# Sliding-window attention followed by a two-matrix feed-forward layer: w_in's first columns in smaller pieces, w_out's products spread over more slots, and 512-token blocks in the middle of the loop

## The chip, the cores and the metric

The kernel runs on one core of a Trainium2 chip. A core has engines that run side by side, each with its own instruction queue: TensorE (PE in the profile; PEld is its weight load), VectorE (DVE), ScalarE (ACT), GpSimd (POOL) and SyncE (SP). They meet through semaphores. POOL, SP and ACT also issue DMA transfers. The metric is device time in microseconds (us), the median of several runs. Before the change it is 308.66 us (three runs, 308.59 to 308.95).

## What is computed

`q`, `k`, `v` have 8 batches, 8 heads, 576 positions and head size 64. The attention output, as 4608 tokens of 512 features, goes through two matrices with an activation between them.

```python
def _attn_ref(q, k, v):                       # window = 32, scale = 1 / sqrt(64)
    scores = scale * np.matmul(q, k.transpose(0, 1, 3, 2))
    mask = np.abs(pos[:, None] - pos[None, :]) <= window
    scores = np.where(mask, scores, -1000000000.0)
    attn = np.exp(scores - np.max(scores, axis=-1, keepdims=True))
    attn = attn / (np.sum(attn, axis=-1, keepdims=True) + 1e-09)
    return np.matmul(attn, v)

def _moe_ref(x, w_in, w_out):                 # w_in 512 x 2048, w_out 2048 x 512
    h = x @ w_in
    g = np.where(h >= 1, h, np.where(h <= -1, 0.0, (h + 1) ** 2 / 4))
    return g @ w_out
```

All inputs and the output are float32; the kernel computes its matmuls in bfloat16 and accumulates in float32.

## The kernel before, in words

**Tokens and slots.** The 4608 tokens are 18 blocks of 256 (`TB`), the 2048 hidden features 8 groups of 256 (`NF`). The main loop (L492) goes through 144 *slots* `a`, with block `t = a // 8` and feature group `f = a % 8`. A slot projects its block onto its 256 features: `project` (L484 to L489), eight matmuls of 256 columns into one PSUM tile `hp` (`[128, 2, 256]`, two feature halves). ACT makes `rr = relu(0.5 h + 0.5)` (L520), DVE `mx = max(h, rr)` (L527) and `gT = min(rr, 1) * mx` (L528), the activated features in bfloat16. (Seven early slots do one of the three steps on ACT.) `hp` has two buffers, `rr` and `mx` three, `gT` a tile per block from a pool of three.

**Second matrix.** `quarter(x)` (L426) does a quarter of a 128-token output tile: four matmuls over four of the 16 feature chunks, 512 columns wide. After the fourth quarter ACT copies the PSUM tile to `osb` and SP issues the store. In slot `a` from 18 on, quarter `a - 8` stands after the projection; eight slots more (144 to 151) finish. The first two blocks go through `pair` (L454), in two column halves, since w_out arrives in two halves; the last tile is split into two column halves too (L429 to L441).

**Attention.** Each batch takes five *sessions*, placed into slots by the list `sl` (L410, L411) through `at`. A session is `sums` (weighted values and row sums for a part of the rows that were scored before; L266) followed by `scores` or `scores8` of the next part (L212, L239), all in 64 x 64 matmuls. ACT takes the exponential of the scores (L236, L261), DVE applies the band mask (L202), ACT makes the reciprocal of the sums by Ln and Exp (L300, L301), and DVE multiplies it in and writes `xT` (L306, L309). That multiplication is put off by `flush` to the start of the next slot's DVE work. `xT` is a ring of four batches (2304 tokens). Within a batch the five sessions sum, in order: two head halves below column 224, two from there to column 480, and the tail (480 to 575).

**Order.** The order on every engine is that of the program (`manual_schedule`); semaphores are put in for data and buffers. Around slot `a`: `flush`, the projection, ACT and DVE on it, the session if there is one (`run(a)`), the quarter. So PE's stream is projection, session, products, and ACT's is `rr`, exp, Ln, Exp, a copy if a tile ended, next `rr`.

**Loads.** Everything from HBM but the first `q` is loaded by POOL, with the cast to bfloat16 in the transfer, in the order of L122 to L158: first k, v of batch 0, w_in's columns 0 to 511 as two transfers (one for each half of the partitions), the second halves of q and k of batch 0, w_in's later columns, w_out's first half, batch 1, the mask copies, w_out's second half, batch 2. At most eight of POOL's transfers are out at a time: an issue waits on the landing of the eighth before it. Batches from 3 on are loaded from slot `sl[...] - 17` on (L417 to L422), and SP transposes their q and k by DMA six and eight slots later (`xpose`, L193). A batch's q goes into the buffer that the k of the batch before leaves free, so its load waits for that transpose.

Of the kernel before, what the change touches and what calls it, by code (L numbers as in the profile page):

```python
# [14 lines left out]
def kernel(  # L15
# [19 lines left out]
    nc = tc.nc  # L35
# [6 lines left out]
    TAIL = S - MAIN  # L42
    RING = 4 * S
    PAD = 32
    LONG = 2

    const = ctx.enter_context(tc.tile_pool(name="const", bufs=1))
# [2 lines left out]
    ptp = ctx.enter_context(tc.tile_pool(name="ptp", bufs=2))  # L50
    smp = ctx.enter_context(tc.tile_pool(name="smp", bufs=2))
    ewp = ctx.enter_context(tc.tile_pool(name="ewp", bufs=3))
    gtp = ctx.enter_context(tc.tile_pool(name="gtp", bufs=3))
    osp = ctx.enter_context(tc.tile_pool(name="osp", bufs=3))
    ps_h = ctx.enter_context(tc.tile_pool(name="ps_h", bufs=2, space=bass.MemoryType.PSUM))
    ps_s = ctx.enter_context(tc.tile_pool(name="ps_s", bufs=1, space=bass.MemoryType.PSUM))
# [11 lines left out]
    w_in = const.tile([128, 4, DFF], BF, name="w_in")  # L68
    w_out = const.tile([128, 16, DM], BF, name="w_out")
    xT = const.tile([128, NY, RING], BF, name="xT")  # L70
    qTs = [const.tile([128, PAD + NY * S], BF, name=f"qT{i}") for i in range(3)]

    ctx.enter_context(tc.manual_schedule())
# [69 lines left out]
    def put(todo):  # L143
        for fn, *x in todo:
            fn(*x)

    cuts = [0, 512, 768, 1024, 1280, 1792, DFF]
    w = [(load_w_in, c0, c1, h) for c0, c1 in zip(cuts, cuts[1:]) for h in range(2)]
    put(w[:2] + [(load_half, 1, t, h) for t in range(2) for h in range(2)] + w[2:10])
    put([(load_w_out, 0, 0, 4)] + w[10:])  # L150
    put([(load_w_out, 0, k, k + 4) for k in range(4, 16, 4)] + [(load_rows, 1, t) for t in range(2)])
    put([(load_v, 1, n) for n in range(4)])
    P.tensor_copy(band[HD[1], 0:128], band[HD[1], 64:192])
# [253 lines left out]
        at(a, seq[2 + n][0])  # L407
    for n, a in enumerate((18, 20, 26.5, 28)):
        at(a, seq[3 + n][1])
    sl = [30, 32, 35, 39, 42, 45, 49, 52, 56, 59, 62, 65, 69, 73, 77, 81, 84, 88, 92]  # L410
    sl += [96, 99, 103, 106, 110, 113, 116, 120, 124, 128]  # L411
    for n, a in enumerate(sl):
        at(a, seq[6 + n][0], seq[7 + n][1] if n < len(sl) - 1 else None)
    for t in range(2):
# [6 lines left out]
        for t in range(2):  # L421
            xps.setdefault(a + 6 + 2 * t, []).append((b, t))  # L422

    gT, op = {}, {}

    def quarter(x):  # L426

        tt, ff = divmod(x, 4)
        if tt == NT // 128 - 1:  # L429
            half, n = divmod(ff, 2)  # L430
            if n == 0:
                op[tt] = ps_o.tile([128, 256], FP, name="op", tag="op")
            cols = slice(256 * half, 256 * half + 256)
            for j in range(NF * n, NF * n + NF):
                nc.tensor.matmul(op[tt], gT[tt // 2][:, j, 128 * (tt % 2):128 * (tt % 2) + 128], w_out[:, j, cols],  # L435
                                 start=j == 0, stop=j == 2 * NF - 1)
            if n:
                osb = osp.tile([128, 256], FP, name="osb")
                A.copy(osb, op[tt])
                nc.sync.dma_start(out=out[128 * tt:128 * tt + 128, cols], in_=osb)  # L440
            return  # L441
        if tt not in op:
            op[tt] = ps_o.tile([128, DM], FP, name="op", tag="op"), []
        o, done = op[tt]
        for j in range(4 * ff, 4 * ff + 4):
            nc.tensor.matmul(o, gT[tt // 2][:, j, 128 * (tt % 2):128 * (tt % 2) + 128], w_out[:, j],  # L446
                             start=not done, stop=len(done) == 2 * NF - 1, skip_group_check=True)
            done.append(j)
        if len(done) == 2 * NF:
            osb = osp.tile([128, DM], FP, name="osb")  # L450
            A.copy(osb, o)  # L451
            nc.sync.dma_start(out=out[128 * tt:128 * tt + 128, :], in_=osb)

    def pair(x):  # L454

        half, p, g = x // 8, x % 8 // 4, x % 4
        if (half, p) not in op:
            op[half, p] = ps_o.tile([128, 2, 256], FP, name="op", tag="op"), []
        o, done = op[half, p]
        for tt in range(2):  # L460
            for j in range(4 * g, 4 * g + 4):
                nc.tensor.matmul(o[:, tt], gT[p][:, j, 128 * tt:128 * tt + 128], w_out[:, j, 256 * half:256 * half + 256],  # L462
                                 start=not done, stop=len(done) == 4 * NF - 1, skip_group_check=True)
                done.append(j)
        if len(done) == 4 * NF:
            osb = osp.tile([128, DM], FP, name="osb")
            A.copy(osb, o.rearrange("p t f -> p (t f)"))
            nc.sync.dma_start(out=out[256 * p:256 * p + 256, 256 * half:256 * half + 256]
                              .rearrange("(t p) f -> p t f", p=128), in_=osb.rearrange("p (t f) -> p t f", t=2))
# [14 lines left out]
    def project(hp, f, r0, todo, first, last):  # L484

        for n, (j, kk) in enumerate(todo):
            nc.tensor.matmul(hp[:, j], w_in[:, kk, 256 * f + 128 * j:256 * f + 128 * j + 128],  # L487
                             xT[:, kk, r0:r0 + TB], start=first and n == 0, stop=last and n == len(todo) - 1,
                             skip_group_check=True)  # L489

    hps = []
    for a in range(NF * NB + NF):  # L492
        t, f = divmod(a, NF)
        eng = None if a < 14 else V
        post = [x for n, x in pairs if n == a] + [a - NF] * (a >= 2 * NF + 2)
        for b, x in loads.get(a, []):
            if x < 2:
                load_nat(b, x)
            else:
                for n in range(4):  # L500
                    load_v(b, n)
        if a == 0 or a > 3:
            flush()
        if t < NB:
            if t not in gT:
                gT[t] = gtp.tile([128, 2 * NF, TB], BF, name="gT", tag="gT")
            r0 = TB * t % RING
            if a in (0,):
                hps = [ps_h.tile([128, 2, TB], FP, name="hp", tag="hp") for _ in range(2)]
                for y in range(2):  # L510
                    for n in range(2):
                        project(hps[n], f + n, r0, [(j, y + 2 * m) for j in range(2) for m in range(2)], y == 0, y == 1)
            elif not hps:
                pool, tag = (ps_o, "op") if a == 6 else (ps_h, "hp")
                hps = [pool.tile([128, 2, TB], FP, name="hp", tag=tag)]
                project(hps[0], f, r0, [(j, kk) for j in range(2) for kk in (0, 2, 1, 3)], True, True)
            hp = hps.pop(0)

            rr = ewp.tile([128, 2, TB], FP, name="rr")
            A.activation(rr, hp, AF.Relu, scale=0.5, bias=0.5)  # L520
            g = gT[t][:, 2 * f:2 * f + 2]
            mx = ewp.tile([128, 2, TB], FP, name="mx")
            if a in two_on_act:
                A.activation(mx, rr, AF.Square)  # L524
                V.scalar_tensor_tensor(g, hp, 1.0, mx, op0=ALU.max, op1=ALU.min)  # L525
            else:
                V.tensor_max(mx, hp, rr)  # L527
                V.scalar_tensor_tensor(g, rr, 1.0, mx, op0=ALU.min, op1=ALU.mult)  # L528
        flush()
        run(a)  # L530
        for x in post:
            (pair if x < 4 * 4 else quarter)(x)
        run(a + 0.5)
        for x in xps.get(a, []):
            xpose(*x)
# [30 lines left out]
```

## Time and profile before

| | |
|---|---|
| median of three runs | 308.66 us |
| the profiled execution | 308.59 us, span 306.8 us |
| PE busy | 298.2 us (97%) |
| DVE busy | 241.2 us (79%) |
| ACT busy | 192.6 us (63%) |
| projections, L487 | 1152 matmuls of 128x256 |
| w_out products, L446 | 496 matmuls of 128x512 |
| granted TensorE clock | 1.000 |

The span is the time from the first to the last instruction of the execution that the profiler took; the time around it (1.8 us) is start and end. In the lists of instructions a line has the start in us, the time from the first start to the last end, engine, line of the source, operation, the tile written `<-` the tiles read, shapes and a count; in brackets the idle time of the engine before it and what ended that. Matmuls overlap: the duration of one is longer than the distance to the next start. Lines of the chain that ended last have a start, the length of the link, and what it was.

### The profile page before, as it was taken

The numbers are of one execution on the slowest core, as the hardware profiler recorded it, in microseconds if no ns is written. First come the engines' busy times: TensorE is split into PE (matmuls) and PEld (weight loads), VectorE is DVE, ScalarE is ACT, GpSimd is POOL, SyncE is SP. The second block draws the span as 40 slices with busy tenths as digits, with TensorE's granted clock in tenths as the row PEclk, the third lists the DMA queues.
The fourth block names the chain that finished last, engine by engine and source line by source line (L and its number), as shares of the span: only waits on it lengthen the run. The fifth ranks groups of instructions, "written<-read, shape, count | busy, mean of one in ns | idle before, by whom it ended". The sixth has DMA issues, their size and how long they took to land.

```text
span 306.8 us, 8482 instructions
## 1 busy us (share of the span) xinstructions
PE 298.2 (97%) x3644; PEld 205.9 (67%) x3644; DVE 241.2 (79%) x376; ACT 192.6 (63%) x320; POOL 76.0 (25%) x90
## 2 busy tenths in 40 slices
PE   7888999999999999999999999999999999999995
PEld 3567878876666666666666666666666666666654
DVE  3278568888888888889888888889888888888760
ACT  3687886738856667666656666566676666554431
POOL 8696661037009006400550002800000000000000
PEclk9999999999999999999999999999999999999999
DMA  9999999999999979996899156990810000010111
GB/s 152 185 198 199 177 200 152 172 156 160 145 184 115 186 149 105 159 92 142 107 166 137 34 107 109 141 157 18 177 49 36 34 36 36 35 36 34 61 44 68
DMA packets 136629, 35.70 MB, mean 116 GB/s; under 512 B 122128, under 2 KB 132368, under 8 KB 136592
## 3 DMA queue, kind: packets, MB, share of 16 engines
q0 software_dynamic: 102432, 18.06, 83.0%
q1 hardware_dynamic: 34016, 16.81, 24.8%
q8 instruction: 28, 0.46, 0.6%
q10 hardware_dynamic: 144, 0.29, 0.3%
q14 instruction: 9, 0.07, 0.1%
HBM read 36.70 MB, written 9.44 MB: 150 GB/s over the span
## 4 chain that ended last, share of the span: by engine, by line
PE 90%; DMA 5%; POOL 3%; ACT 1%; issue 1%; DVE 0%; POOLq 0%; ACTq 0%
PE hp L487 39%; PE op L446 36%; PE bb L294 6%; PE op L462 4%; DMA w_in<-in_moe_w_in_dram 2%; DMA qh<-in_q_dram 2%; PE bb L228 2%; POOL vn L106 1%; PE op L435 1%; POOL w_in L110 1%; PE tp L188 1%; ACT pt L236 1%; POOL kh L85 0%; DVE gT L525 0%; ACT mx L524 0%
## 5 line engine op out<-in xcount | busy, mean ns | idle before, releaser
L487 PE MATMUL hp<-xT,w_in 128*128 128x256 bf16 x1152 | 149.4, 273 | 2.5 <-DMA w_in<-in_moe_w_in_dram 1.5
L520 ACT ACTIVATE rr<-hp 128x512 f32<-128x512 f32 x144 | 85.6, 595 | 87.9 <-PE hp L487 87.8
L487 PEld LDWEIGHTS <-w_in 128*128 128x128 bf16 x1152 | 112.0, 98 | 42.0 <-issue 2.7
L446 PE MATMUL op<-w_out,gT 128*128 128x512 bf16 x496 | 126.9, 380 | 0.0
L527 DVE TENSOR_TENSOR mx<-hp,rr 128x512 f32<-128x512 f32 x137 | 94.5, 690 | 31.0 <-ACT rr L520 29.0
L528 DVE SCALAR_TENSOR_TENSOR gT<-rr,mx 128x512 bf16<-128x512 f32 x137 | 94.8, 692 | 4.7
L446 PEld LDWEIGHTS <-gT 128*128 128x128 bf16 x496 | 46.1, 98 | 34.8
L98 POOL DMA_DIRECT2D qn<-in_q_dram x12 | 14.6, 1221 | 111.8 <-DMA kT<-kn 109.3
L236 ACT ACTIVATE pt<-bb 128x1024 bf16<-128x1024 f32 (+1 forms) x33 | 32.7, 1002 | 4.7 <-PE bb L228 3.4
L306 DVE TENSOR_TENSOR xT<-bb,rc 128x512 bf16<-128x512 f32 (+1 forms) x32 | 21.0, 658 | 10.1 <-ACT rc L301 9.5
L106 POOL DMA_DIRECT2D vn<-in_v_dram x32 | 27.7, 895 | 4.8 <-DMA w_out<-in_moe_w_out_dram 4.0
L301 ACT ACTIVATE rc<-lr 128x512 f32<-128x512 f32 (+2 forms) x40 | 23.5, 587 | 1.3
L451 ACT COPY osb<-op 128x512 f32<-128x512 f32 x31 | 18.1, 583 | 8.7 <-PE op L446 8.3
L300 ACT ACTIVATE lr<-bb 128x512 f32<-128x512 f32 (+2 forms) x40 | 22.0, 551 | 0.4 <-PE bb L294 0.3
L202 DVE TENSOR_TENSOR pt<-pt,mask 128x1024 bf16<-128x1024 bf16 (+1 forms) x33 | 20.3, 614 | 0.5 <-ACT pt L236 0.5
L294 PE MATMUL bb<-pt,ones 64*64 64x256 bf16 (+3 forms) x352 | 19.5, 255 | 0.1
L294 PE MATMUL bb<-pt,vn 64*64 64x128 bf16 (+3 forms) x712 | 18.4, 204 | 0.1
L294 PEld LDWEIGHTS <-vn 64*64 64x64 bf16 x712 | 16.7, 107 | 0.3 <-DMA vn<-in_v_dram 0.3
L462 PE MATMUL op<-w_out,gT 128*128 128x256 bf16 x128 | 16.5, 273 | 0.0
L294 PEld LDWEIGHTS <-ones 64*64 64x64 bf16 x352 | 10.3, 105 | 8.4 <-issue 8.4
L98 POOL DMA_DIRECT2D kn<-in_k_dram x12 | 14.6, 1230 | 0.1
L228 PE MATMUL bb<-qT,kT 64*64 64x128 bf16 (+1 forms) x520 | 13.1, 217 | 0.3 <-DVE kT L191 0.2
(59 smaller groups left out, 110.1 us busy)
## 6 DMA issues: line engine op xcount, KB each, us to landing
out_dram<-osb SPq DMA_DIRECT2D x35, 256.0 KB, 2.4
vn<-in_v_dram POOLq DMA_DIRECT2D x32, 144.0 KB, 10.2
qn<-in_q_dram POOLq DMA_DIRECT2D x12, 288.0 KB, 6.5
kn<-in_k_dram POOLq DMA_DIRECT2D x12, 288.0 KB, 9.1
w_in<-in_moe_w_in_dram POOLq DMA_DIRECT2D x4, 256.0 KB, 5.8
w_in<-in_moe_w_in_dram POOLq DMA_DIRECT2D x8, 128.0 KB, 6.4
w_out<-in_moe_w_out_dram POOLq DMA_DIRECT2D x4, 256.0 KB, 8.7
w_out<-in_moe_w_out_dram POOLq DMA_DIRECT2D x2, 512.0 KB, 13.3
```

The lines of the kernel that those rows point to most:

```text
L98: nc.gpsimd.dma_start(out=x[:, :, h], in_=src[b, NY * h:NY * h + NY].rearrange("y s d -> (y s) d") .rearrange("(u p) d -> p u d", p=128))
L106: nc.gpsimd.dma_start(out=vn[b][64 * a:64 * a + 64, :, h], in_=v[b, y:y + 2].rearrange("y s d -> (y s) d") .rearrange("(c r) d -> r c d", ...
L236: A.activation(p, ps[:, :, :w * n].rearrange(like, y=m), AF.Exp, scale=D ** -0.5)
L294: nc.tensor.matmul(bb[HD[h], a, o + c0:o + c1], ones[HD[a]] if c is None else vn[b][HD[a], c, h], p(a, h), start=n == 0, stop=True, skip_g ...
L300: A.activation(lr[:, :, :D0], bb[:, :, D0:2 * D0], AF.Ln)
L301: A.activation(rc[:, :, :D0], lr[:, :, :D0], AF.Exp, scale=-1.0)
L446: nc.tensor.matmul(o, gT[tt // 2][:, j, 128 * (tt % 2):128 * (tt % 2) + 128], w_out[:, j], start=not done, stop=len(done) == 2 * NF - 1, s ...
L462: nc.tensor.matmul(o[:, tt], gT[p][:, j, 128 * tt:128 * tt + 128], w_out[:, j, 256 * half:256 * half + 256], start=not done, stop=len(done ...
L487: nc.tensor.matmul(hp[:, j], w_in[:, kk, 256 * f + 128 * j:256 * f + 128 * j + 128], xT[:, kk, r0:r0 + TB], start=first and n == 0, stop=l ...
L520: A.activation(rr, hp, AF.Relu, scale=0.5, bias=0.5)
L527: V.tensor_max(mx, hp, rr)
L528: V.scalar_tensor_tensor(g, rr, 1.0, mx, op0=ALU.min, op1=ALU.mult)
```

## The change

Four things change together.

- **w_in.** The list of cuts gets a 256, so columns 0 to 255 and 256 to 511 come as four transfers of 128 KB (counted in bfloat16) where two of 256 KB were; the second halves of q and k still follow them.
- **gT.** The pool is replaced by one tile `gT[128, 16, 4, 256]`: 16 feature chunks, four block *homes*, 256 tokens. Block `t` lives in home `t % 4`; in the wide slots homes 0 and 3 are exchanged, so that the two blocks of a wide slot can be written in one instruction of two runs.
- **Wide slots.** In slots 72 to 135 (blocks 9 to 16) a block has 512 tokens and a slot 128 features: four matmuls of 512 columns where eight of 256 were. ACT's and DVE's instructions keep their size.
- **Order of products and sessions.** `quarter` becomes `unit`, one matmul at a time. From slot 40 on the slots do 4, 3, 3, 4, 3, 3, ... units up to slot 87, and 4 from 88 on, through slot 159. The sessions of `sl` from the ninth on are placed earlier (55, 57, 60, 63, 66, 68, ... where 56, 59, 62, 65, 69, 73, ... stood), with the fifth batch's (batch 4's) tail in slot 68; loads and transposes follow them.

```diff
@@ -42,6 +42,7 @@
     TAIL = S - MAIN
     RING = 4 * S
     PAD = 32
+    WIDE = 72, 136
     LONG = 2
 
     const = ctx.enter_context(tc.tile_pool(name="const", bufs=1))
@@ -50,7 +51,6 @@
     ptp = ctx.enter_context(tc.tile_pool(name="ptp", bufs=2))
     smp = ctx.enter_context(tc.tile_pool(name="smp", bufs=2))
     ewp = ctx.enter_context(tc.tile_pool(name="ewp", bufs=3))
-    gtp = ctx.enter_context(tc.tile_pool(name="gtp", bufs=3))
     osp = ctx.enter_context(tc.tile_pool(name="osp", bufs=3))
     ps_h = ctx.enter_context(tc.tile_pool(name="ps_h", bufs=2, space=bass.MemoryType.PSUM))
     ps_s = ctx.enter_context(tc.tile_pool(name="ps_s", bufs=1, space=bass.MemoryType.PSUM))
@@ -68,6 +68,7 @@
     w_in = const.tile([128, 4, DFF], BF, name="w_in")
     w_out = const.tile([128, 16, DM], BF, name="w_out")
     xT = const.tile([128, NY, RING], BF, name="xT")
+    gT = const.tile([128, 16, 4, 256], BF, name="gT")
     qTs = [const.tile([128, PAD + NY * S], BF, name=f"qT{i}") for i in range(3)]
 
     ctx.enter_context(tc.manual_schedule())
@@ -144,10 +145,10 @@
         for fn, *x in todo:
             fn(*x)
 
-    cuts = [0, 512, 768, 1024, 1280, 1792, DFF]
+    cuts = [0, 256, 512, 768, 1024, 1280, 1792, DFF]
     w = [(load_w_in, c0, c1, h) for c0, c1 in zip(cuts, cuts[1:]) for h in range(2)]
-    put(w[:2] + [(load_half, 1, t, h) for t in range(2) for h in range(2)] + w[2:10])
-    put([(load_w_out, 0, 0, 4)] + w[10:])
+    put(w[:4] + [(load_half, 1, t, h) for t in range(2) for h in range(2)] + w[4:12])
+    put([(load_w_out, 0, 0, 4)] + w[12:])
     put([(load_w_out, 0, k, k + 4) for k in range(4, 16, 4)] + [(load_rows, 1, t) for t in range(2)])
     put([(load_v, 1, n) for n in range(4)])
     P.tensor_copy(band[HD[1], 0:128], band[HD[1], 64:192])
@@ -407,8 +408,8 @@
         at(a, seq[2 + n][0])
     for n, a in enumerate((18, 20, 26.5, 28)):
         at(a, seq[3 + n][1])
-    sl = [30, 32, 35, 39, 42, 45, 49, 52, 56, 59, 62, 65, 69, 73, 77, 81, 84, 88, 92]
-    sl += [96, 99, 103, 106, 110, 113, 116, 120, 124, 128]
+    sl = [30, 32, 35, 39, 42, 45, 49, 52, 55, 57, 60, 63, 66, 68, 72, 76, 79, 82, 86]
+    sl += [90, 93, 96, 100, 104, 108, 111, 114, 118, 123]
     for n, a in enumerate(sl):
         at(a, seq[6 + n][0], seq[7 + n][1] if n < len(sl) - 1 else None)
     for t in range(2):
@@ -421,34 +422,35 @@
         for t in range(2):
             xps.setdefault(a + 6 + 2 * t, []).append((b, t))
 
-    gT, op = {}, {}
-
-    def quarter(x):
-
-        tt, ff = divmod(x, 4)
+    op = {}
+
+    def home(t):
+
+        return (3 - t % 4 if t % 4 in (0, 3) else t % 4) if WIDE[0] <= NF * t < WIDE[1] else t % 4
+
+    def unit(x):
+
+        tt, j = divmod(x, 16)
         if tt == NT // 128 - 1:
-            half, n = divmod(ff, 2)
+            half, n = divmod(j, 8)
             if n == 0:
                 op[tt] = ps_o.tile([128, 256], FP, name="op", tag="op")
             cols = slice(256 * half, 256 * half + 256)
-            for j in range(NF * n, NF * n + NF):
-                nc.tensor.matmul(op[tt], gT[tt // 2][:, j, 128 * (tt % 2):128 * (tt % 2) + 128], w_out[:, j, cols],
-                                 start=j == 0, stop=j == 2 * NF - 1)
-            if n:
+            for k in (2 * n, 2 * n + 1):
+                nc.tensor.matmul(op[tt], gT[:, k, home(tt // 2), 128 * (tt % 2):128 * (tt % 2) + 128], w_out[:, k, cols],
+                                 start=k == 0, stop=k == 15)
+            if n == 7:
                 osb = osp.tile([128, 256], FP, name="osb")
                 A.copy(osb, op[tt])
                 nc.sync.dma_start(out=out[128 * tt:128 * tt + 128, cols], in_=osb)
             return
-        if tt not in op:
-            op[tt] = ps_o.tile([128, DM], FP, name="op", tag="op"), []
-        o, done = op[tt]
-        for j in range(4 * ff, 4 * ff + 4):
-            nc.tensor.matmul(o, gT[tt // 2][:, j, 128 * (tt % 2):128 * (tt % 2) + 128], w_out[:, j],
-                             start=not done, stop=len(done) == 2 * NF - 1, skip_group_check=True)
-            done.append(j)
-        if len(done) == 2 * NF:
+        if j == 0:
+            op[tt] = ps_o.tile([128, DM], FP, name="op", tag="op")
+        nc.tensor.matmul(op[tt], gT[:, j, home(tt // 2), 128 * (tt % 2):128 * (tt % 2) + 128], w_out[:, j],
+                         start=j == 0, stop=j == 15)
+        if j == 15:
             osb = osp.tile([128, DM], FP, name="osb")
-            A.copy(osb, o)
+            A.copy(osb, op[tt])
             nc.sync.dma_start(out=out[128 * tt:128 * tt + 128, :], in_=osb)
 
     def pair(x):
@@ -459,7 +461,7 @@
         o, done = op[half, p]
         for tt in range(2):
             for j in range(4 * g, 4 * g + 4):
-                nc.tensor.matmul(o[:, tt], gT[p][:, j, 128 * tt:128 * tt + 128], w_out[:, j, 256 * half:256 * half + 256],
+                nc.tensor.matmul(o[:, tt], gT[:, j, p, 128 * tt:128 * tt + 128], w_out[:, j, 256 * half:256 * half + 256],
                                  start=not done, stop=len(done) == 4 * NF - 1, skip_group_check=True)
                 done.append(j)
         if len(done) == 4 * NF:
@@ -489,10 +491,11 @@
                              skip_group_check=True)
 
     hps = []
-    for a in range(NF * NB + NF):
-        t, f = divmod(a, NF)
+    done = 4 * (40 - NF)
+    for a in range(NF * NB + 2 * NF):
+        wide = WIDE[0] <= a < WIDE[1]
         eng = None if a < 14 else V
-        post = [x for n, x in pairs if n == a] + [a - NF] * (a >= 2 * NF + 2)
+        post = [] if a >= 40 else [x for n, x in pairs if n == a] + [a - NF] * (a >= 2 * NF + 2)
         for b, x in loads.get(a, []):
             if x < 2:
                 load_nat(b, x)
@@ -501,24 +504,33 @@
                     load_v(b, n)
         if a == 0 or a > 3:
             flush()
-        if t < NB:
-            if t not in gT:
-                gT[t] = gtp.tile([128, 2 * NF, TB], BF, name="gT", tag="gT")
-            r0 = TB * t % RING
-            if a in (0,):
-                hps = [ps_h.tile([128, 2, TB], FP, name="hp", tag="hp") for _ in range(2)]
-                for y in range(2):
-                    for n in range(2):
-                        project(hps[n], f + n, r0, [(j, y + 2 * m) for j in range(2) for m in range(2)], y == 0, y == 1)
-            elif not hps:
-                pool, tag = (ps_o, "op") if a == 6 else (ps_h, "hp")
-                hps = [pool.tile([128, 2, TB], FP, name="hp", tag=tag)]
-                project(hps[0], f, r0, [(j, kk) for j in range(2) for kk in (0, 2, 1, 3)], True, True)
-            hp = hps.pop(0)
+        if a < NF * NB:
+            if wide:
+                n, f = divmod(a - WIDE[0], 2 * NF)
+                t = WIDE[0] // NF + 2 * n
+                r0 = TB * t % RING
+                hp = ps_h.tile([128, 2, TB], FP, name="hp", tag="hp")
+                for n, kk in enumerate((0, 2, 1, 3)):
+                    nc.tensor.matmul(hp.rearrange("p n t -> p (n t)"), w_in[:, kk, 128 * f:128 * f + 128],
+                                     xT[:, kk, r0:r0 + 2 * TB], start=n == 0, stop=n == 3)
+                g = gT[:, f, home(t):home(t + 1) + 1:home(t + 1) - home(t)]
+            else:
+                t, f = divmod(a, NF)
+                r0 = TB * t % RING
+                if a in (0,):
+                    hps = [ps_h.tile([128, 2, TB], FP, name="hp", tag="hp") for _ in range(2)]
+                    for y in range(2):
+                        for n in range(2):
+                            project(hps[n], f + n, r0, [(j, y + 2 * m) for j in range(2) for m in range(2)], y == 0, y == 1)
+                elif not hps:
+                    pool, tag = (ps_o, "op") if a == 6 else (ps_h, "hp")
+                    hps = [pool.tile([128, 2, TB], FP, name="hp", tag=tag)]
+                    project(hps[0], f, r0, [(j, kk) for j in range(2) for kk in (0, 2, 1, 3)], True, True)
+                hp = hps.pop(0)
+                g = gT[:, 2 * f:2 * f + 2, home(t)]
 
             rr = ewp.tile([128, 2, TB], FP, name="rr")
             A.activation(rr, hp, AF.Relu, scale=0.5, bias=0.5)
-            g = gT[t][:, 2 * f:2 * f + 2]
             mx = ewp.tile([128, 2, TB], FP, name="mx")
             if a in two_on_act:
                 A.activation(mx, rr, AF.Square)
@@ -529,7 +541,16 @@
         flush()
         run(a)
         for x in post:
-            (pair if x < 4 * 4 else quarter)(x)
+            if x < 16:
+                pair(x)
+            else:
+                for j in range(4):
+                    unit(4 * x + j)
+        if a >= 40:
+            n = (4, 3, 3)[a % 3] if a < 88 else 4
+            for x in range(done, done + n):
+                unit(x)
+            done += n
         run(a + 0.5)
         for x in xps.get(a, []):
             xpose(*x)
```

## The prediction

> **What bounds the kernel now.** I read the page first (shares, chain that ended last), then PE's waits, then three stretches of the timeline: a plain stretch, one with an attention session, and the start. A *slot* below is one turn of the main loop (one `hp` tile), a *session* the attention matmuls put into a slot.
>
> ```profile
> span 306.8 us, 8482 instructions
> PE 298.2 (97%) x3644; PEld 205.9 (67%) x3644; DVE 241.2 (79%) x376; ACT 192.6 (63%) x320; POOL 76.0 (25%) x90
> PE 90%; DMA 5%; POOL 3%; ACT 1%; issue 1%; DVE 0%; POOLq 0%; ACTq 0%
> ```
>
> PE is the chain but for 10%, and that 10% lies in the first 34 us. So a change pays what it takes off PE's stream, plus or minus what it does to the start, plus any wait it makes for PE.
>
> ```profile
> 273.70 1.04 PE L487 MATMUL hp<-xT,w_in 128*128 128x256 bf16 x8
> ...
> 294.54 1.04 PE L487 MATMUL hp<-xT,w_in 128*128 128x256 bf16 x8
> ...
> 295.58 4.32 PE op L446 x20
> ```
>
> The first two lines are the starts of the projections of slots 131 and 143: twelve slots in 20.84 us, 1.7367 us each. The last (from the chain) is 20 matmuls of 512 columns: 4.32/20 = 0.216 us each. Four of them are 0.864, so the eight 256-column matmuls of a projection take 0.8727, 109.1 ns each. (The "273 ns" of the page is one matmul's latency, not its spacing.)
>
> ```profile
> 220.27 0.40 PE L228 MATMUL bb<-qT,kT 64*64 64x128 bf16 x16
> 220.72 1.02 ACT L236 ACTIVATE pt<-bb 128x1024 bf16<-128x1024 f32 x1 [0.17 <-PE bb L228]
> 221.47 1.04 PE L487 MATMUL hp<-xT,w_in 128*128 128x256 bf16 x8
> 221.64 0.59 ACT L300 ACTIVATE lr<-bb 128x512 f32<-128x512 f32 x1
> 222.26 0.63 ACT L301 ACTIVATE rc<-lr 128x512 f32<-128x512 f32 x1
> 222.80 0.57 ACT L451 COPY osb<-op 128x512 f32<-128x512 f32 x1
> 222.93 0.69 DVE L306 TENSOR_TENSOR xT<-bb,rc 128x512 bf16<-128x512 f32 x1 [0.32 <-ACT rc L301]
> 223.27 0.60 ACT L520 ACTIVATE rr<-hp 128x512 f32<-128x512 f32 x1
> 223.90 0.69 DVE L527 TENSOR_TENSOR mx<-hp,rr 128x512 f32<-128x512 f32 x1 [0.28 <-ACT rr L520]
> 224.95 1.04 PE L487 MATMUL hp<-xT,w_in 128*128 128x256 bf16 x8
> ```
>
> This is the session of slot 103, the tightest place after slot 40. Its scores end, ACT does exp, Ln, Exp, an output copy, and only then `rr` of slot 104; DVE's `mx` of slot 104 ends at 224.59. With two `hp` buffers, slot 106's projection (224.95) needs that `mx`: slack 0.36 us. The slack before the next-but-two projection, read the same way at every session, is by its place in the batch: tail sums 1.06; the two with cut 224: 0.91; first with the upper range 0.73; second 1.08. Where an output copy lies in the session's slot it falls to 0.57 (slot 39), 0.46 (59, 99) and 0.36 (103). PE never waits from slot 40 on.
>
> ```profile
> 14.87 2.55 POOL L110 DMA_DIRECT2D w_in<-in_moe_w_in_dram  x4 [0.77 <-DMA qh<-in_q_dram]
> 17.90 1.03 PE L487 MATMUL hp<-xT,w_in 128*128 128x256 bf16 x8 [0.65 <-DMA w_in<-in_moe_w_in_dram]
> 24.12 1.03 PE L487 MATMUL hp<-xT,w_in 128*128 128x256 bf16 x8 [0.80 <-DMA w_in<-in_moe_w_in_dram]
> 20.00:21.00 1.00, 1.00 (x12) 0.65 (x14) 0.97 (x2) 1.00 (x3) 1.00 (x3) 1.00 1.23 203
> 23.00:28.00 5.00, 4.20 (x86) 3.52 (x73) 4.39 (x9) 4.13 (x9) 3.30 (x4) 1.00 1.45 195
> ```
>
> At the start PE waits for w_in at slots 2 and 5; the last figure of the two stretches is GB/s: the DMA engines run full, at 203 while 512-column pieces of w_in move and 195 on 256-column pieces. What comes after the first piece is a queue at that rate.
>
> **Part 1, 512-token blocks (slots 72 to 135).** Each of 64 slots gives up eight 256-column matmuls (0.8727 us) for four of 512 (0.864, by the w_out rows): 0.0087 x 64 = **-0.56 us**. Only those 256 matmuls and weight loads go: ACT and DVE still do 512 columns a slot, the weight loads were hidden (98 ns under 109). Bounds: 0 if 512 columns cost two times 256; -0.6 at most. Both sides write one 512-column PSUM tile per slot, and the last matmul ends as late (0.65 + 0.38 against 0.76 + 0.27). I take -0.56 because the w_out matmuls are the same shape on the same data type.
>
> The Trainium skill (TensorE: Matmul & The Clock Gate, "Back-to-back issue gap") gives a sustained 131 ns per matmul at 512 columns, and 216 as the gap of an isolated one. By 131 a projection would fall to 0.524 us and the kernel to an estimated 286 us. The 20 matmuls in 4.32 us are a sustained stream and take 216, so the measurement decides.
>
> **Part 2, w_in pieces.** Columns 0 to 511 come as four transfers instead of two. POOL issues two more (626 ns each), which moves the qh/kh loads' issue from 7.84 to about 9.1 us; their data moves only after w_in's, from about 12.4 us, so the issue is hidden, and the w_in issue of 14.87 waits on the qh landing as now. 512 KB at 195 instead of 203 GB/s is 2.69 against 2.58 us: everything queued behind moves by **+0.10 us**, at 17.90 and again at 24.12, from where PE runs on. The earlier first half buys nothing: the projections of slot 0 are released at 13.41 and 14.70 by DVE's `xT`, not by w_in. Bounds: -0.1 (the first piece frees a place in the queue early) to +0.6 (one issue on the path). The mask copies and every later load are two POOL instructions further down, behind waits on landings.
>
> The Trainium skill (DMA: Bandwidth & Descriptors, "Measured") says to batch to 1 MiB and has 341 GB/s there against 138 at 64 KB. An estimate by these, 512 KB at 138 instead of 341, is 2.3 us lost. The trace's 203 and 195 with transfers queued back to back speak for the small figure.
>
> **Part 3, w_out products deferred.** From slot 40 to 87 a slot does 4, 3, 3 of them instead of 4, later 4 again; 16 slots instead of 8 remain after slot 143, each four matmuls of 0.216 as now. The sum on PE is the same: 0. But a slot without a session falls to 0.873 + 3.33 x 0.216 = 1.59 us. Between a session and the projection that needs its `mx` stand three sets of products, now 10 instead of 12: every slack shrinks by 2 x 0.216 = 0.43. Without a copy 0.63, 0.48, 0.30, 0.65 remain, no wait. Copies now end tiles in slots 44, 49, 54, 59, 63, 68, 73, 78, 83, 87; with sessions they meet in 49, 63 (0.36 - 0.43 = -0.07) and 68 (0.57 - 0.43 = 0.14). The two negative ones, with 0.06 us that PE needed after a DVE release at 33.87, wait 0.14 each: **+0.28 us**. Behind the waiting projection stand that slot's products, which nobody needs soon. Bounds: 0, and 15 sessions in 42 to 86 at 0.14 = 2.1.
>
> DVE's load is the warning: slots 52 to 71 now hold seven sessions. PE: 20 x 0.873 + 66 x 0.216 + sessions of 0.75 to 0.90 (by slot-to-slot starts), together 5.55 = 37.3 us. DVE: 20 x 1.382 + masks 4.1 + `xT` 4.4 = 36.1 us, 97%, a little less since its instructions overlap by some 0.04. It fits, barely.
>
> **Part 4, sessions earlier, loads with them.** Sessions only change place: 0. Distances of two slots (55 to 57, 66 to 68) leave 2 x 0.873 + 6 x 0.216 = 3.0 us from scores to the next sums; the tail's `xT` there ends about 2.7 us after the scores, scores8's 2.5. The wide block of slot 72 needs session 68, four slots ahead; slot 120 needs session 118, whose `xT` ends 2.5 us after the scores while the third matmul, the first to read it, comes at 3.0. SP's transposes for the fifth batch move to about 123 and 133 us, their first use (slot 68) is at about 148. All 0, with 0.5 for slot 120 as the far end.
>
> **Part 5, one gT tile of four homes.** DVE now writes two runs of 256 apart instead of 512 in a row. The `xT` row writes two such runs, in 692 ns, as `gT` does in 692: 0. A home is written again only when its products were issued slots before: 0.
>
> **Sum.** 308.59 (the profiled execution: span 306.8 and 1.8 around it) - 0.56 + 0.10 + 0.28 = 308.41; the median of the three runs is 0.07 above that execution: **308.5 us**. Under 0.2% (0.62 us) a measurement can hardly tell this kernel from an unchanged one.
>
> **Rivals.**
> - *Slower: PE waits for `mx` at most sessions of 40 to 87.* For it: the 97% and slacks of 0.3 to 0.5 that one more ACT copy or a DVE backlog eats. Against: by hand each backlog (0.2 to 0.4 us at a session) ends before the next `xT`, as ACT's `rc` comes later. At the full 2.1 us: 310.3. It decides from 1.1 us of waits, 0.07 a session. Chance 0.18.
> - *Faster: no waits, and the start gains.* For it: 0.87 us of PE idle before 24.12. Against: a full DMA queue. With 0.3 gained at the start: 308.66 - 0.56 - 0.3 = 307.8. Chance 0.15.
> - *Late transposes for slot 68.* Margin 10 us against landings of 4.6 to 13.0; beyond it PE idles: a miss of 3 us gives 311.5. Chance 0.03.
> - *The wide matmul saves nothing.* 308.66 + 0.10 + 0.28 = 309.0. Against: the 512-column row. Chance 0.05.
>
> **How the numbers follow.** The forecast has 0.59; with the last rival it makes 0.64 for within 0.2% (308.04 to 309.28). Faster 0.15, slower 0.18 + 0.03 = 0.21. The range goes from 307.8 (no waits, start gains) to 309.8 (about two thirds of the 2.1 us), leaving out some 0.05 below and 0.12 above.
>
> **What will show it.** Starts of wide slots after 125 1.728 us apart (wrong: 1.737 or more). Slot 5's projection at 24.2. PE waiting for `mx` at slots 52 and 66 by 0.1 to 0.2 and hardly elsewhere; DVE near 97% in slots 52 to 71. The forecast is wrong if PE's waits for DVE sum to over 1 us, or if slot 5 starts 0.5 us off.

## The result and the profile after

The changed kernel took **307.98 us** (median of six runs, 307.84 to 308.18) against 308.90 for the kernel before beside it: ratio 0.9973, 95% interval 0.996 to 0.9986. Two later sets on other occasions were closer: 308.17 against 308.77 (0.9986, 0.9978 to 0.9995) and 308.17 against 308.62 (0.9987, 0.9978 to 0.9995). All its 28 runs together have the median 308.15, all 102 of the kernel before 308.69. So the change is worth about **0.55 us, 0.18%**; the first six runs flattered it.

The page of the changed kernel (span and instructions; busy time by engine; shares of the chain that ended last):

```profile
span 306.1 us, 7974 instructions
PE 298.4 (97%) x3388; PEld 181.2 (59%) x3388; DVE 239.6 (78%) x376; ACT 191.2 (62%) x320; POOL 77.1 (25%) x92
PE 91%; POOL 3%; DMA 2%; ACT 1%; issue 1%; DVE 0%; POOLq 0%; ACTq 0%
```

PE is still the bound. Its 256 fewer matmuls do not show in its busy time, since that is made of overlapping durations; distances between starts show them. The first of the last five wide slots (131 to 135) and slot 136 behind them, from PE's timeline of the changed kernel (start, time to the last end, engine, line, operation):

```profile
266.19 1.03 PE L514 MATMUL hp<-xT,w_in 128*128 128x512 bf16 x4
...
274.82 1.04 PE L489 MATMUL hp<-xT,w_in 128*128 128x256 bf16 x8
```

These are five steps in 8.63 us, 1.726 each (1.7266 over the eleven from slot 125 on), where slots took 1.7367 before: 0.0101 a slot, **0.65 us** over 64 slots.

The session of slot 49, with everything on `hp`, `xT` and the output copy, from the timeline of all engines:

```profile
113.76 1.04 PE L489 MATMUL hp<-xT,w_in 128*128 128x256 bf16 x8
114.09 0.69 DVE L540 SCALAR_TENSOR_TENSOR gT<-rr,mx 128x512 bf16<-128x512 f32 x1
115.28 1.04 PE L489 MATMUL hp<-xT,w_in 128*128 128x256 bf16 x8
115.31 0.56 ACT L453 COPY osb<-op 128x512 f32<-128x512 f32 x1
115.44 0.69 DVE L307 TENSOR_TENSOR xT<-bb,rc 128x512 bf16<-128x512 f32 x1
115.77 1.18 ACT L533 ACTIVATE rr<-hp 128x512 f32<-128x512 f32 x2
115.90 0.33 SPq L454 DMA_DIRECT2D out_dram<-osb  x1
116.41 0.69 DVE L539 TENSOR_TENSOR mx<-hp,rr 128x512 f32<-128x512 f32 x1 [0.28 <-ACT rr L533]
117.13 0.69 DVE L540 SCALAR_TENSOR_TENSOR gT<-rr,mx 128x512 bf16<-128x512 f32 x1
117.15 1.03 PE L489 MATMUL hp<-xT,w_in 128*128 128x256 bf16 x8
```

The copy of 115.31 stands before `rr` on ACT; so `rr` comes late, `mx` ends at 117.10, and slot 52's projection starts 0.05 us behind it, at 117.15. It stands 1.87 us after slot 51's (115.28), where four products allow 1.74: **0.13 us** of waiting. Slot 66 does the same after the copy in 63: `mx` ends at 143.43, the projection starts at 143.48 (1.65 after slot 65 where three products allow 1.52, 0.13). No other slot from 40 on is late.

The start. First the projections of slots 0 and 1 in the kernel before, then PE's lines on `hp` before 24 us of the changed kernel:

```profile
13.41 1.03 PE L487 MATMUL hp<-xT,w_in 128*128 128x256 bf16 x8 [0.46 <-DVE xT L306]
14.70 1.03 PE L487 MATMUL hp<-xT,w_in 128*128 128x256 bf16 x8 [0.26 <-DVE xT L306]
```

```profile
13.24 0.60 PE L489 MATMUL hp<-xT,w_in 128*128 128x256 bf16 x4 [0.44 <-DVE xT L307]
14.50 1.47 PE L489 MATMUL hp<-xT,w_in 128*128 128x256 bf16 x12 [0.67 <-DMA w_in<-in_moe_w_in_dram]
18.53 1.03 PE L489 MATMUL hp<-xT,w_in 128*128 128x256 bf16 x8 [0.72 <-DMA w_in<-in_moe_w_in_dram]
23.84 1.03 PE L489 MATMUL hp<-xT,w_in 128*128 128x256 bf16 x8
```

Slots 0 and 1 are projected together (16 matmuls); the last twelve wait for w_in's columns 256 to 511. Slot 2 is 0.63 us later than before, yet slot 5 is 0.28 earlier (24.12 before). Where nothing holds slot 5 it follows slot 4 by 1.51 us (the experiments with a cut at 1536 below); here slot 4 is at 22.18, so slot 5 waited 0.15, too little for the view to name.

PE's last matmul ends at 302.73 (before: 303.39). From slot 5's start to there: 278.89 against 279.27. So this execution gained 0.66 us: 0.65 by wide matmuls, less 0.26 for two waits, and 0.28 at the start.

### The profile page after: what moved, and what is told of

Read it like the earlier page. It is cut to its first block, busy times and chain, and to the rows that moved or that the text cites. A ratio compares the mean times of both kernels' runs of the same rounds, so it can differ in the third digit from the quotient of the medians.

```text
span 306.1 us, 7974 instructions
## 1 busy us (share of the span) xinstructions
PE 298.4 (97%) x3388; PEld 181.2 (59%) x3388; DVE 239.6 (78%) x376; ACT 191.2 (62%) x320; POOL 77.1 (25%) x92
## 4 chain that ended last, share of the span: by engine, by line
PE 91%; POOL 3%; DMA 2%; ACT 1%; issue 1%; DVE 0%; POOLq 0%; ACTq 0%
PE op L449 36%; PE hp L489 22%; PE hp L514 18%; PE bb L295 6%; PE op L464 4%; PE bb L229 2%; DMA w_in<-in_moe_w_in_dram 2%; POOL vn L107 1%; PE op L440 1%; POOL w_in L111 1%; PE tp L189 1%; ACT pt L237 1%; POOL kh L86 1%; POOL qh L86 0%; PE bb L208 0%
## 5 line engine op out<-in xcount | busy, mean ns | idle before, releaser
L489 PE MATMUL hp<-xT,w_in 128*128 128x256 bf16 x640 | 83.1, 273 | 2.2 <-DMA w_in<-in_moe_w_in_dram 1.4
L489 PEld LDWEIGHTS <-w_in 128*128 128x128 bf16 x640 | 61.8, 98 | 22.7 <-issue 2.8
L514 PE MATMUL hp<-xT,w_in 128*128 128x512 bf16 x256 | 65.7, 379 | 0.0
L514 PEld LDWEIGHTS <-w_in 128*128 128x128 bf16 x256 | 25.0, 98 | 30.2
L99 POOL DMA_DIRECT2D qn<-in_q_dram x12 | 14.6, 1224 | 89.5 <-DMA kT<-kn 87.4
## 6 DMA issues: line engine op xcount, KB each, us to landing
w_out<-in_moe_w_out_dram POOLq DMA_DIRECT2D x2, 512.0 KB, 13.2
```

The lines of the kernel that those rows point to most:

```text
L514: nc.tensor.matmul(hp.rearrange("p n t -> p (n t)"), w_in[:, kk, 128 * f:128 * f + 128], xT[:, kk, r0:r0 + 2 * TB], start=n == 0, stop=n == 3)
```

## The experiments

The question was the start. **Theory A**: the pieces and the order of the loads bring it forward. **Theory B**: fetches of PE's own instructions through the DMA engines move it, from run to run and by where they fall. Beside that, the other two terms of the sum that are not zero, the wide slots and the waits, were taken out alone.

What B rests on was read from the landings and the DMA packets in the trace. A transfer lands in sixteen increments; PE is released by the last. The page counts a queue that the program does not issue; its columns are packets, MB, and share of 16 DMA engines' span (first the kernel before, then the changed one):

```profile
q8 instruction: 28, 0.46, 0.6%
```
```profile
q8 instruction: 26, 0.43, 0.6%
```

The kernel without wide slots (below), which has the 256 matmuls and their weight loads back, has 28 again. The packets are 16 KB each and take 0.88 to 1.9 us, while half of the data packets around 20 us take 0.06. Two of them fall before slot 5. The sixteen landings of the second half of columns 1280 to 1791, which slot 5 needs (us from the span's start; "fetch" is the second packet's start):

```
run               fetch   8th     14th    15th    last    slot 5
before            21.40   22.36   22.74   23.04   23.99   24.12
changed           22.27   22.38   22.80   22.89   23.70   23.84
changed, again    21.75   22.54   22.86   23.41   23.94   24.07
changed, third    22.11   22.48   22.95   23.68   24.12   24.25
more instructions 18.55   22.79   23.28   23.89   24.02   24.16
two pieces        22.74   22.55   23.17   23.65   24.78   24.91
```

Over these rows the eighth landing moves by 0.43 us and slot 5 by 1.07; the last landing is 1.2 to 2.2 us behind the eighth, and slot 5 follows the last within 0.15.

### Two pieces again, and pieces alone

The changed kernel with columns 0 to 511 in two transfers:

```diff
-    cuts = [0, 256, 512, 768, 1024, 1280, 1792, DFF]
+    cuts = [0, 512, 768, 1024, 1280, 1792, DFF]
...
-    put(w[:4] + [(load_half, 1, t, h) for t in range(2) for h in range(2)] + w[4:12])
-    put([(load_w_out, 0, 0, 4)] + w[12:])
+    put(w[:2] + [(load_half, 1, t, h) for t in range(2) for h in range(2)] + w[2:10])
+    put([(load_w_out, 0, 0, 4)] + w[10:])
```

> The changed kernel with w_in's columns 0 to 511 in two transfers again. In the trace of the changed kernel slot 5's projection starts at 23.84 us (24.12 before) and slot 2's at 18.53 (17.90 before). Theory A, the smaller pieces move the landings: with two pieces slot 2 goes back to 17.9 and slot 5 to 24.1, the time to about 308.25 us. Theory B, one of the 16 DMA engines is held for about 0.9 us by a 16 KB fetch of PE's instructions, and which transfer lands late by that depends on where the fetch falls: the median landing of each transfer stays within 0.1 us, the fetches near 12 and 22 us stay, and slot 5's start goes with the last of the 16 engines, anywhere from 23.3 to 24.2; the time between 307.4 and 308.4. By both the rest (wide slots, two waits of 0.13 at slots 52 and 66) is as in the changed kernel.

> The two-piece kernel once more (the changed kernel with w_in's columns 0 to 511 in two transfers again). From slot 5 on 278.88. Theory A: 0.4 below the kernel before. Theory B: the same 0.4 below the kernel before, and level with the changed kernel.

Measured: 308.36 (307.66 to 311.12; ratio 0.9998, 0.998 to 1.0016) and 308.35 (307.96 to 310.42; 1.0002, 0.9986 to 1.0017). The intervals are wide because four of the 23 runs, 309.64 to 311.12 us, had a mean granted clock of 0.992 to 0.994, where the others had 0.998 or more. In the first profile (308.97 us) slot 2 is at 18.52 and slot 5 at 24.91, later than either theory had it. The second profile (309.64 us) is of one of the four. PE's timeline of it, and the row of the stretch from 16 to 19 us, in which the third figure from the end is the granted clock:

```profile
14.89 2.70 PE L489 MATMUL hp<-xT,w_in 128*128 128x256 bf16 x16 [1.98 <-DMA w_in<-in_moe_w_in_dram]
19.45 1.05 PE L489 MATMUL hp<-xT,w_in 128*128 128x256 bf16 x8
25.10 1.05 PE L489 MATMUL hp<-xT,w_in 128*128 128x256 bf16 x8
16.00:19.00 3.00, 3.00 (x36) 2.26 (x36) 1.47 (x3) 1.94 (x4) 3.00 (x6) 0.50 1.41 189
```

All sixteen matmuls of slots 0 and 1 stand until 14.89: the second transfer's 13th increment lands at 13.10, its last at 14.76, with a fetch of 0.94 us at 12.69. Behind that the clock stood at 0.50, so slots 2 and 5 are late by the clock too, and only the start of slot 0 can be compared with other profiles. What starts such a drop is not shown: PE stood idle almost as long (1.77 to 1.92 us) in three other profiles with two transfers, at a clock of 1.00. Both profiled executions are slower than this kernel's median, so they overstate what its start usually loses.

The other way round, the kernel before with only the four pieces (the same edit reversed):

> The kernel before with only w_in's first columns in four transfers. Theory A (pieces): slot 2 at 18.5 us, slot 5 at 23.84, 308.4 us or 0.27 below the kernel before. Theory B (instruction fetch): medians of the landings as before, slot 5 anywhere from 23.3 to 24.5 by where the fetch falls; from slot 12 to the end every distance as before. My forecast's step of +0.10 us would show as slot 5 at 24.2.

> The kernel before with only the four pieces, once more. From slot 5 on 279.28. Theory A: 0.2 to 0.3 below the kernel before. Theory B: within 0.1 of it.

Measured: 308.66 (ratio 0.9996, 0.9987 to 1.0005) and 308.71 (1.0007, 0.9995 to 1.0019); slot 5 at 24.20 and 24.03. Slot 5 at 24.20 is where the forecast's +0.10 would put it, 24.03 is not. In the kernel before the first fetch does not hold w_in back: the last increment of columns 0 to 511 lands at 13.21, and slots 0 and 1 start at 13.41. With four pieces it does not in the first profile (last increment 13.33, start 13.33), but in the second it does: the last increment lands at 13.99, 0.67 us behind the 15th, and twelve of the sixteen matmuls wait for it:

```profile
14.12 1.53 PE L487 MATMUL hp<-xT,w_in 128*128 128x256 bf16 x12 [0.20 <-DMA w_in<-in_moe_w_in_dram]
```

### The changed kernel again

> The changed kernel itself once more, beside the kernel before on the same chip. Theory A (the four pieces and the order of the loads bring the start forward by 0.27 us): slot 5's projection at 23.84 again, within 0.1, in every profiled execution, and a median of 307.98 within 0.1. Theory B (the start is decided by which of the sixteen DMA engines is held by a fetch of PE's instructions when the last piece that slot 5 needs lands): slot 5 anywhere between 23.8 and 24.3, median 307.9 to 308.3. Both: from slot 5's start to the last matmul's end 278.89 us, as in the first profile of this kernel.

> The changed kernel a third time, so that its runs can be set beside the two-piece kernel's on the same chip. From slot 5 on 278.88 us, as in both profiles so far. Theory A (the new front of the loads is worth 0.2 to 0.3 us): its median lies 0.2 to 0.3 below that of the two-piece kernel and 0.6 to 0.7 below that of the kernel before. Theory B (the front is worth nothing and the start only scatters): it lies within 0.1 of the two-piece kernel and 0.3 to 0.5 below the kernel before.

Measured: 308.17 both times, slot 5 at 24.07 and 24.25, and 278.88 us from there to the last matmul's end both times, as in the first profile. So in this kernel's three profiles nothing after slot 5 varies, and the 23.84 of the first profile was an early one; theory A's 23.84 in every execution did not come, and by these profiles alone (24.12 in the one of the kernel before) no gain at the start would show. Against the two-piece kernel on the same chip the third set is 0.18 lower, between what the theories had. All runs pooled: 308.15 (28 runs, none above 309.3) against 308.36 (23 runs, four above 309.3), a difference of 0.2 (95% interval 0.08 to 0.45, by resampling the runs; 0.17, 0.05 to 0.33, without the four runs of lower clock); for the kernel before 308.69 (102 runs) against 308.70 with pieces (23 runs, interval of the difference -0.19 to 0.09). The pieces are worth some 0.2 us in the changed kernel and nothing that shows in the one before.

### More instructions, the same time on PE

```diff
-        for _ in range(n):
-            nc.tensor.matmul(z, warm[:, :128], warm, start=True, stop=True)
+        for m in range(n if n < 11 else 4 * n):
+            s = slice(0, 512) if n < 11 else slice(128 * (m % 4), 128 * (m % 4) + 128)
+            nc.tensor.matmul(z[:, s], warm[:, :128], warm[:, s], start=True, stop=True)
```

> The changed kernel, but the eleven matmuls of 512 columns that stand before the first attention work are written as forty-four of 128 columns: the same time on PE, 66 instructions more, so that PE's queue comes to each later instruction fetch earlier in its program. Theory A (fetches do not matter): slot 2 at 18.5 and slot 5 at 23.84 as in the changed kernel, within 0.1. Theory B (a fetch of 16 KB holds one DMA engine for nearly 1 us, and whatever transfer it meets lands late by that): the fetch that stood at 22.27 lies over 1 us earlier, the last landing of the piece for slot 5 moves with it, and slot 5 or slot 2 moves by 0.2 to 0.9 in either direction; from slot 5 to the end 278.9.

Measured: 308.24 (ratio 0.9985, 0.9969 to 1.0). The second fetch moved to 18.55, so the queue does carry PE's instructions. With it the second late increment, which in the changed kernel first shows in the piece for slot 5, now shows already in columns 1024 to 1279: 14th landing 20.48, 15th 21.32, last 21.42, where the changed kernel has 20.07, 20.13, 21.11. Slot 2 is at 18.84 and slot 5 at 24.16, both 0.3 later than in the changed kernel's first profile. From slot 5 to the end it took 279.14, not 278.9; from slot 12 on it is 266.17, as in the changed kernel (266.16). So the late increments moved with the fetch, as B has it, in the one execution profiled. B's price of 0.2 to 0.9 is not shown: slot 5 lies within what the changed kernel's own executions differ by (23.84 to 24.25).

### No wide slots

`WIDE = 72, 136` becomes `200, 200`: no slot is wide; all else stays.

> The changed kernel with no wide slots: all 144 slots have 256 tokens and eight matmuls of 256 columns; products, sessions, gT and w_in as changed. If the wide slots are worth what their spacing shows (1.7266 against 1.7368 us a slot, 64 slots) the time rises by 0.65 us over the changed kernel, to about 308.6, and slots 125 to 135 are 1.737 apart. If their worth lies elsewhere (waits that they remove or make), the rise is under 0.3 or over 1.0.

Measured: 308.82 (ratio 1.0001, 0.9993 to 1.001), 0.67 above the changed kernel's pooled 308.15. Slots 128 and 136 in PE's timeline:

```profile
262.07 1.04 PE L489 MATMUL hp<-xT,w_in 128*128 128x256 bf16 x8
...
275.96 1.04 PE L489 MATMUL hp<-xT,w_in 128*128 128x256 bf16 x8
```

Eight steps in 13.89 us, 1.736 each, as before the change. From slot 125 to 136 it takes 19.10 us, the changed kernel 18.99: 0.0100 a slot. From slot 5 to the end it takes 279.52, 0.64 more than the changed kernel. The 0.65 is confirmed by spacing, by that stretch and by medians, and without it no gain shows.

### Copies out of the session slots

```diff
-            n = (4, 3, 3)[a % 3] if a < 88 else 4
+            n = {48: 3, 49: 2, 50: 5, 63: 3, 64: 4, 68: 2, 69: 5}.get(a, (4, 3, 3)[a % 3] if a < 88 else 4)
```

> The changed kernel with the products of slots 48 to 50 dealt 3, 2, 5 (4, 3, 3 there), 63 and 64 dealt 3, 4 (4, 3) and 68 and 69 dealt 2, 5 (3, 4), so that no output copy falls into the slot of a session of 49, 63 or 68. Theory, the two waits of 0.13 at slots 52 and 66 come from ACT's copy ahead of rr: both go, and the time falls by 0.26 us to about 307.7. Rival, DVE's load of 97% in slots 52 to 71 makes them: they stay or move to a slot near by, and the time stays at 308.0.

Measured: 308.09 (ratio 0.9979, 0.997 to 0.9988). The same stretch as above, of this kernel:

```profile
115.38 0.58 ACT L533 ACTIVATE rr<-hp 128x512 f32<-128x512 f32 x1
115.57 1.04 PE L489 MATMUL hp<-xT,w_in 128*128 128x256 bf16 x8
115.86 0.58 ACT L453 COPY osb<-op 128x512 f32<-128x512 f32 x1
116.11 0.68 DVE L539 TENSOR_TENSOR mx<-hp,rr 128x512 f32<-128x512 f32 x1
117.30 1.04 PE L489 MATMUL hp<-xT,w_in 128*128 128x256 bf16 x8
```

The copy now follows the `rr` that mattered, `mx` ends at 116.79, and slot 52 has 0.51 us to spare; slot 51 to 52 is 1.74, and slot 65 to 66 is 1.52. From slot 5 to the end it takes 278.63, 0.26 less. At slot 52 this edit did a second thing: slots 49 to 51 hold eleven products where they held ten, and one more (0.216 us) would by itself cover a wait of 0.13. Slot 66 has no such doubt: slots 63 to 65 hold ten products in both kernels, only the copy's place differs, and `mx` ends at 143.21, 0.30 before the projection. The median alone would not show the gain: it is 0.06 below the changed kernel's, and the 307.7 that was expected did not come.

### A cut at 1536, and the two mends together

In the first, the changed kernel has two transfers at the front and slot 5 waits for half as much:

```diff
-    cuts = [0, 256, 512, 768, 1024, 1280, 1792, DFF]
+    cuts = [0, 512, 768, 1024, 1280, 1536, 1792, DFF]
...
-    put(w[:4] + [(load_half, 1, t, h) for t in range(2) for h in range(2)] + w[4:12])
+    put(w[:2] + [(load_half, 1, t, h) for t in range(2) for h in range(2)] + w[2:12])
```

> The changed kernel, but slots 0 and 1 share one pair of transfers again (columns 0 to 511) and the pair of columns 1280 to 1791 is cut at 1536, so that slot 5 waits for 128 KB instead of 256 KB in each of the two. Theory A (the pieces at the front are what brought the start forward): slot 0 at 14.9 as in the two-piece kernel, slot 2 at 18.5, slot 5 no earlier than 24.0; 308.1 to 308.4. Theory B (the landing of the last piece that slot 5 needs sets its start): that piece lands some 1.3 us earlier, slot 5 does not wait for it and starts when PE has done slot 4, 23.2 to 23.8; 307.4 to 308.0. From slot 5 to the end 278.9 in both.

Measured: 308.19 (ratio 0.9986, 0.9974 to 0.9998). Slot 5's piece lands whole at 22.50 and nothing waits for it, as B had; but slot 5 starts at 24.19, as A had. Slots 0 and 1 began at 14.77, the transposes of k behind them came late, and between slots 2 and 3 (2.14 us apart, 1.70 in the changed kernel) PE waited 0.20 for DVE's `kT`; so the delay came down the stream. From slot 5 to the end it took 279.05. With the copies moved as well:

> Both mends together: the products dealt out so that no output copy falls into the slots of the sessions 49 and 63 (which removed both waits in the run before this one), and the pieces cut at 1536. If the two add: from slot 5 to the end 278.63, slot 5 at 23.2 to 23.8, 307.1 to 307.7, faster than the changed kernel by 0.3 to 0.8. If the start does not gain (slot 5 at 24.0 or later): 307.8 to 308.1.

Measured: 307.88 (ratio 0.9971, 0.9956 to 0.9986), slot 0 at 14.83 and slot 5 at 24.24: the start gained nothing, the waits are gone (265.91 from slot 12 on). The last one keeps the four pieces, cuts at 1536 and moves the copies:

> The changed kernel with the products dealt out so that no output copy falls into the slots of the sessions 49 and 63, the four pieces at the front kept, and the pair of columns 1280 to 1791 cut at 1536 as well. From slot 5 on 278.63. Slot 0 at 13.2 to 13.5 as in the changed kernel; slot 5 does not wait for its piece any more and starts by slot 2's landing of 18.3 to 18.8, so at 23.6 to 24.1, without the later values that the changed kernel's runs imply. Median 307.4 to 307.9. If the extra pair of transfers costs what the forecast took for a split (0.1 on everything queued behind), 0.1 more.

Measured: **307.79** (307.44 to 308.09; ratio 0.9968, 0.9951 to 0.9986). PE's timeline:

```profile
13.44 0.60 PE L489 MATMUL hp<-xT,w_in 128*128 128x256 bf16 x4 [0.45 <-DVE xT L307]
18.73 1.03 PE L489 MATMUL hp<-xT,w_in 128*128 128x256 bf16 x8 [0.66 <-DVE gT L537]
23.89 1.05 PE L489 MATMUL hp<-xT,w_in 128*128 128x256 bf16 x8
```

Slot 5 waits for no transfer. In this execution 0.37 us of the early start were lost again by slot 12, so from slot 5 on it takes 279.00, not 278.63; from slot 12 on it is the 0.25 shorter (265.91 against 266.16). It is the fastest of all, 0.38 below the changed kernel on the same chip; from the kernel without the four pieces (0.09) its runs do not separate it.

## Why the prediction was right or wrong

- **Wide matmuls.** Forecast -0.56, measured -0.65. The term mis-sized is "Four of them are 0.864", the 0.216 us of a w_out matmul. In the wide slots eight 512-column matmuls take 1.7266, 215.8 ns each. 1.7367 less eight of those is 0.0101 a slot instead of 0.0087: 0.2 ns, rounded up eight times a slot. The sustained 131 ns of the Trainium skill (TensorE: Matmul & The Clock Gate, "Back-to-back issue gap") is as far away in these slots as it was in the w_out stream: 64 slots of sustained 512-column matmuls stay at 216.
- **Waits for `mx`.** Forecast two, of 0.14, at slots 52 and 66; measured two, of 0.13, there and nowhere else. The reason, an output copy ahead of `rr` in a session's slot, was shown by moving the copies, at slot 66 with nothing else changed. DVE's load in slots 52 to 71 came to 34.71 of 37.40 us, 93% where 97% was worked out by adding durations that overlap; the rival of waits at most sessions did not come.
- **The start.** Forecast +0.10, measured -0.28 in the first profiled execution, but -0.05 and +0.13 in the two others. By medians it is 0.55 less 0.38 from slot 5 on, about -0.16. The step that failed: "The earlier first half buys nothing: the projections of slot 0 are released at 13.41 and 14.70 by DVE's `xT`, not by w_in." That holds for the kernel before, and pieces alone moved its slot 5 by 0.08 and -0.09 in two profiles and its median by nothing. With the new loop, four profiles with two transfers at the front all have w_in's last increment for slots 0 and 1 at 14.6 to 14.8, and both slots wait; with four transfers the first four of their sixteen matmuls go at 13.2 to 13.5 and the rest at 14.4 to 14.9. So there the earlier first half does buy something, 0.2 us by medians. That the rest of the new program brings the late increment with it is likely (all eleven profiles of the new loop have it, one of three of the old), not shown; by medians the two-piece kernel's start loses only some 0.05 against the kernel before.
- **The 0.10 itself.** No run shows it. It came from 203 and 195 GB/s, read as the rates of 512- and 256-column pieces, but the stretch from 23 to 28 us also has w_out and q in its queue. The eighth landing of slot 5's piece stands at 22.36 to 22.55 in three profiles with two transfers and at 22.38 to 22.62 in seven with four (22.79 with more instructions).
- **Sessions, transposes, the split `gT` write.** Forecast 0. From slot 5 on the whole difference, -0.38, is -0.65 + 0.26, which leaves nothing for them; for slot 68 and slot 120 nothing is late, and `gT` takes 692 ns in the wide slots too. They were not taken out alone.
- **The sum.** Forecast 308.5, that is 0.16 below the median then known; measured 0.55 below over all runs. The missing 0.4 are 0.26 at the start, 0.09 from the wide matmuls, 0.02 from the waits: three errors of one sign, and the time is in the range although the start went the other way. The faster rival named 307.8 by "no waits, and the start gains": the start gained, half of what it named; the waits came.
- **Open.** Why the first fetch holds w_in's columns 0 to 511 in every profile of the new loop and in one of three of the old is not settled: it starts at 11.9 to 12.5 there and at 12.1 to 12.7 here. The packets there take 0.89 us in the three profiles with the old loop and 0.89 to 0.98 with the new one; which of the sixteen DMA engines they hold is not in the trace.

## What to carry to other kernels

Where PE waits for a queue of transfers, look at the last of the sixteen landings, not the median: a small piece that lets part of the work start is cheap insurance against one late increment (some 0.2 us in the changed kernel, nothing that shows in the one before). Tell a deterministic stretch (here 278.88 us, three times) from a scattering start before reading tenths of a microsecond out of six runs. Where an engine's order is written out by hand, keep a copy that nobody awaits from standing ahead of the one step that a buffer's return depends on.

## What was not expected of the hardware

PE's instructions come through the DMA engines in packets of 16 KB that take 0.88 to 1.9 us each (26 packets in the changed kernel, 28 in the kernels with 512 matmuls and weight loads more). While the queue of loads is full, the transfers behind such a packet land fifteen increments on time and one late, and this goes on from transfer to transfer: in the changed kernel's first profile the last increment is 0.8 to 1.1 us behind the 15th from the second half of columns 256 to 511 (13.40 and 14.37) up to slot 5's piece. Sixty-six instructions more ahead of it moved such a packet by 3.7 us. So the length of a program, even of its early part alone, moves the moment at which the last increments of its first weights land; what that is worth could not be told here from the scatter of the start.
